# A linear-attention and gated-FFN kernel on one core: new engine orders, PSUM banks, engine choices and weight-load order, with the same operations

## The chip, the cores and the metric

The kernel runs on one core of one Trainium2 chip. The metric is the device time of one execution in microseconds (us), as the median of several runs of the same program. TensorE (PE in the profile, with PEld for its weight loads) multiplies matrices into PSUM. PSUM is used as eight banks of 128 x 512 f32. VectorE (DVE), ScalarE (ACT) and GpSimd (POOL) do elementwise work, and SyncE (SP) issues DMAs. Each engine takes its own list of instructions strictly in order and waits on semaphores for what other engines or DMAs must have done.

## The reference

Two layers follow each other. The first is a recurrence over 768 tokens for each of 4 batches and 8 heads of width 48. The second is a gated feed-forward layer (FFN) on the 3072 tokens of width 384 that come out of it, with a hidden width of 1536.

```python
f = 1.0 / (1.0 + np.exp(-f_logit))
for t in range(S):
    state = f[:, :, t, :, None] * state + np.einsum('bhd,bhe->bhde', k[:, :, t], v[:, :, t])
    y[:, :, t] = np.einsum('bhd,bhde->bhe', q[:, :, t], state)
x = y.transpose(0, 2, 1, 3).reshape(B * S, H * D)
out = (np.maximum(x @ w_gate, 0.0) * (x @ w_val)) @ w_out
```

Inputs and outputs are f32; the kernel multiplies in bf16.

## The kernel before, in words

**Units.** The tokens are cut into 12 units of 256 tokens: unit u is one batch and one pair of 128-token chunks (called y = 0 and 1), and units 0 to 3 are the first pair of the four batches, 4 to 7 the second, 8 to 11 the third. For each unit `unit` (the block from line 545 on) does the recurrence in chunks:

- four loads from DRAM, f, k, q and v, 384 KB each, issued by SyncE (`load`, DMA on line 468), into a ring of four buffers per input;
- on ScalarE the exponential (L546) and logarithm (L550, or L555 without the sum) of the gate, for some units a sum of pairs on GpSimd or VectorE (L552), then cumulative sums as matmuls (`cum`, L560 to 564) and exponentials of those (L577, L580, L587);
- the "hats", k and q times these exponentials (L599 for whole tiles in units 0 to 3, L605 for half tiles in the others);
- bf16 copies of v into `vpad` (L622; named v00, v01, v10, v11 by chunk and half) and, in units 0 to 3, into `vrest` (L626; named r0, r1). A copy goes through `copy_on`, whose line in the profile tells the engine: L402 ScalarE, L403 VectorE or GpSimd, L400 a reduction over one element on VectorE;
- the transposes of the hats: on TensorE for units 0 to 3 (L637, one for k, one for q, each with a copy out of PSUM, L643, named tk and tq), by two DMA transposes on SyncE's queue for units 4 to 11 (L648);
- the scores (L662) with their masks: on VectorE straight from PSUM (L676), or on ScalarE and then GpSimd (L671, L673);
- the decay of the state (L699 to 708, or through small DMAs in later units), the state matmuls k times v (L717 in units 4 to 11, L727 in 0 to 3), and the new state (L513, or L517 on VectorE and L520 on GpSimd);
- the output of each chunk, directly in transposed form (L760, copy named x0 or x1 into `xT`, L782) or in natural form (L767, L771) with a DMA transpose (L790).

**FFN.** Two units give a group of 512 tokens, that is four token tiles; there are six groups. `ffn_hidden` does one 128-wide slice j of the hidden layer: three matmuls with `wg` and three with `wv` (one line, L811), the relu on ScalarE (L816), the product on VectorE (L823). I call the three matmuls on one weight, with one PSUM tile, a matmul group. In the first two FFN groups the slices 0 to 5 are done for token tiles 0 and 1 and for tiles 2 and 3 apart, 256 columns each; all else has 512 columns. `ffn_out` multiplies by `wo` (L841, 12 matmuls to a token tile), copies out of PSUM (named o0 or o1) and stores (L862, SyncE). The last token tile is done in two cuts of columns, 256 and 128.

**Weights.** Each of the three weights is loaded in four slices of three 128-wide blocks, by DMAs that GpSimd issues (`load_w`, L482) and that cast from f32 to bf16. wg0 and wv0 hold what hidden slices 0 to 2 need, wg1 and wv1 slices 3 to 5, and so on. `FIRST` (L276) lists all loads of the start; a name after @ is a load that must have landed before the weight's DMA is issued (its release). Between the weights' issues GpSimd does its elementwise work in the order of its list.

**The order.** Nothing is scheduled at run time. The program adds 1088 operations, numbered 0 to 1087 in the order of the code. `SEQUENCE` (L184) gives, for each engine, the operations in the order in which it takes them; `HOMES` (L233) gives the PSUM tiles that each of the eight banks holds, one after the other; `UNITS` (L261) gives the engine of each elementwise operation of a unit. `Plan.link` finds what depends on what, `Plan.follow` lays the tiles into the banks, so that a tile's first matmul waits for the last reader of the tile before it, and `Plan.needs` works out the semaphore waits. `FILLERS` (L259) names TensorE operations that are preceded by matmuls on zeros, into a bank that is free at that time: (count of 512 columns, bank, columns of one more). `run` (L904) emits each engine's list.

Operations to which the lists below and the steps refer:

| number | what it is |
|---|---|
| 67, 68 / 105, 106 | cumulative sums of unit 0 / 1 on TensorE |
| 83, 85 / 121, 123 | transposes of k and q of unit 0 / 1; 84, 86 and 122, 124 are the copies tk, tq |
| 77 to 82 | v00, v01, r0, v10, r1, v11 of unit 0; 115 to 120 the same of unit 1 |
| 87, 90 / 125, 128 / 264, 268 | scores of unit 0 / 1 / 2 |
| 95, 134, 436 | state matmuls of unit 0, 1, 4 |
| 96, 99 / 135, 138 | outputs of unit 0 / 1 on TensorE; 97, 100 and 136, 139 their copies x0, x1 |
| 131 | the mask of unit 1 on GpSimd (L673) |
| 53, 54, 55, 56, 57 | the issues of wg0, wv0, wg1, wv1, wg2 (up to 60: wv2, wg3, wv3) |
| 146, 154 / 174, 178 | first hidden groups on tiles 0 and 1 / on tiles 2 and 3 |
| 194 | the first matmul group on wg2 (hidden slice 6) |
| 145, 424, 425 | v load of unit 4, and its two DMA transposes (L648) |
| 1083, 1086 | the last matmul group of the kernel and the last copy out of PSUM |

Of the kernel before, what the change touches and what calls it, by code (L numbers as in the profile page):

```python
# [38 lines left out]
class Plan:  # L39
# [91 lines left out]
    def needs(self):  # L131
# [127 lines left out]
FILLERS = {67: (9, 0, 448), 105: (6, 0, 320), 85: (0, 1, 448), 87: (2, 1, 256), 123: (2, 7, 0), 95: (1, 2, 0)}  # L259
# [23 lines left out]
def bass_hgrn2_outer__then__ffn_reglu_kernel(  # L283
# [601 lines left out]

    for n in FILLERS:
        pl.ops[n].reads.append("zeros")
# [73 lines left out]
```

## Time and profile before

| | |
|---|---|
| median of three runs | 187.22 us (186.69 to 187.68) |
| the profiled execution | 186.4 us |
| its span, first to last instruction | 185.1 us |
| granted TensorE clock | 1.00 |
| HBM read, written | 25.96 MB, 4.73 MB |
| DMA queues: SyncE's (q1), GpSimd's (q0) | 29.09 MB, 3.54 MB |

The span is what the profiler saw between the first and the last instruction; the 1.3 us to the execution's time lie outside it. The page lists for each engine its busy time, its share of the span and its count of instructions; the groups are by source line, with "xN" the count, then the summed busy time, the mean in ns of one, and the idle time of the engine just before them with what ended most of it. In the chain of waits each row is a start in us from the span's start, a duration, the engine, the tile and the line. In the list of instructions each row is a start and a duration too. In the table by stretches the numbers of each engine are its busy us and its count of instructions in that stretch. A wait is written reader, arrow, what ended it, then the summed idle us, the count and the largest.

### The profile page before, as it was taken

What the parts mean: (1) busy time and instruction counts of PE and PEld (TensorE: products, weight loads), DVE (VectorE), ACT (ScalarE), POOL (GpSimd) and SP (SyncE); (2) the same over time, 40 slices, a digit from 0 to 9 for tenths busy, and PEclk for the clock granted to TensorE, in tenths of its full rate; (3) what the DMA queues carried; (4) which work ended last, traced back from release to release, by engine and by line L of the source; (5) the groups of instructions that cost most, each with busy time, mean ns of one, the idle gap of its engine ahead of it and who ended that gap; (6) DMA issues with size and microseconds to landing.
All of it is one profiled execution on the core that took longest, in us unless ns stands there. A gap on an engine that the chain in (4) does not pass through costs nothing.

```text
span 185.1 us, 4315 instructions
## 1 busy us (share of the span) xinstructions
PE 180.1 (97%) x1689; PEld 102.9 (56%) x1689; DVE 126.1 (68%) x239; ACT 120.4 (65%) x242; POOL 101.2 (55%) x133
## 2 busy tenths in 40 slices
PE   7998998999999999999999999999999999999995
PEld 2454885476676556445565444656545566444564
DVE  3389775978488998999778696862865642335521
ACT  4999857889766888977786586266753641446112
POOL 5279903899949837979639998233670270000000
PEclk9999999999999999999999999999999999999999
DMA  5999999959999999979998998997028104000053
GB/s 153 323 325 267 226 204 205 251 123 175 197 302 202 211 264 289 242 162 262 266 230 159 261 258 188 234 172 178 17 67 217 22 4 106 0 0 4 0 212 127
DMA packets 83167, 32.89 MB, mean 178 GB/s; under 512 B 75334, under 2 KB 83148, under 8 KB 83148
## 3 DMA queue, kind: packets, MB, share of 16 engines
q1 hardware_dynamic: 78348, 29.09, 65.1%
q0 software_dynamic: 4800, 3.54, 12.7%
q8 instruction: 13, 0.21, 0.5%
q14 instruction: 6, 0.05, 0.1%
HBM read 25.96 MB, written 4.73 MB: 166 GB/s over the span
## 4 chain that ended last, share of the span: by engine, by line
PE 88%; SPq 3%; DVE 3%; DMA 3%; ACT 2%; issue 1%
PE ps L811 50%; PE ps L841 26%; SPq L468 3%; PE ps L662 3%; DMA k_in<-in_k_dram 3%; PE ps L760 2%; DVE ptm L676 1%; PE ps L771 1%; PE ps L717 1%; PE ps L767 1%; PE ps L637 1%; PE ps L562 1%; PE ps L727 1%; ACT relu L816 1%; DVE hats L599 1%
## 5 line engine op out<-in xcount | busy, mean ns | idle before, releaser
L823 DVE TENSOR_TENSOR gT<-relu,ps 128x512 bf16<-128x512 bf16 (+1 forms) x84 | 50.1, 625 | 24.6 <-PE ps L811 18.1
L816 ACT ACTIVATE relu<-ps 128x512 bf16<-128x512 f32 (+1 forms) x84 | 42.8, 537 | 29.1 <-PE ps L811 20.5
L811 PE MATMUL ps<-xT,wv 128*128 128x512 bf16 (+1 forms) x252 | 55.4, 349 | 0.0
L811 PE MATMUL ps<-xT,wg 128*128 128x512 bf16 (+1 forms) x252 | 54.6, 349 | 0.5 <-ACT f_in L550 0.5
L841 PE MATMUL ps<-wo,gT 128*128 128x384 bf16 (+2 forms) x300 | 53.7, 320 | 0.0
L841 PEld LDWEIGHTS ps<-wo,gT 128*128 128x128 bf16 x300 | 27.9, 98 | 18.0
L811 PEld LDWEIGHTS ps<-xT,wg 128*128 128x128 bf16 x252 | 23.2, 98 | 20.9 <-ACT f_in L550 0.8
L811 PEld LDWEIGHTS ps<-xT,wv 128*128 128x128 bf16 x252 | 23.3, 98 | 19.9 <-ACT relu L816 0.5
L673 POOL TENSOR_TENSOR ptm<-ptm,seen 128x512 bf16<-128x512 bf16 x21 | 24.0, 1156 | 18.1 <-ACT ptm L671 17.5
L605 POOL TENSOR_TENSOR hats<-q_in,expo 64x384 bf16<-64x384 f32 x28 | 27.8, 994 | 10.1 <-ACT expo L580 6.8
L676 DVE TENSOR_TENSOR ptm<-ps,seen 128x512 bf16<-128x512 f32 x27 | 17.5, 684 | 2.8 <-PE ps L662 2.6
L605 DVE TENSOR_TENSOR hats<-k_in,ps 64x384 bf16<-64x384 f32 x32 | 17.6, 551 | 0.9 <-DMA k_in<-in_k_dram 0.3
L520 POOL TENSOR_TENSOR st<-ssum,dec 128x384 bf16<-128x384 f32 x16 | 13.1, 832 | 5.5 <-DVE ssum L517 5.4
L671 ACT ACTIVATE ptm<-ps 128x512 bf16<-128x512 f32 x21 | 11.6, 595 | 6.0 <-PE ps L662 6.0
L403 DVE COPY osb<-ps 128x384 f32<-128x384 f32 (+2 forms) x15 | 7.9, 530 | 8.7 <-PE ps L841 8.4
L580 ACT ACTIVATE expo<-ps 128x384 f32<-128x384 f32 x22 | 9.9, 490 | 3.9 <-DVE ps L569 3.8
L403 POOL CAST vpad<-v_in 64x384 bf16<-64x384 f32 x20 | 10.4, 522 | 2.9 <-DMA v_in<-in_v_dram 1.8
L402 ACT ACTIVATE osb<-ps 128x384 f32<-128x384 f32 x10 | 4.9, 492 | 10.9 <-PE ps L841 10.9
L546 ACT ACTIVATE f_in<-f_in 128x768 f32<-128x768 f32 x12 | 10.1, 844 | 2.0 <-DMA f_in<-in_f_logit_dram 2.0
L402 ACT ACTIVATE vpad<-v_in 64x384 bf16<-64x384 f32 x21 | 10.9, 519 | 0.3
L552 POOL TENSOR_TENSOR bneg<-f_in 128x384 bf16<-128x384 f32 x7 | 7.0, 999 | 6.7 <-ACT f_in L550 6.6
L517 DVE TENSOR_TENSOR ssum<-ps,st 128x384 f32<-128x384 f32 x16 | 8.9, 554 | 2.2 <-PE ps L717 1.8
(90 smaller groups left out, 176.8 us busy)
## 6 DMA issues: line engine op xcount, KB each, us to landing
f_in<-in_f_logit_dram SPq DMA_DIRECT2D x12, 384.0 KB, 4.8
k_in<-in_k_dram SPq DMA_DIRECT2D x12, 384.0 KB, 4.8
q_in<-in_q_dram SPq DMA_DIRECT2D x12, 384.0 KB, 4.9
v_in<-in_v_dram SPq DMA_DIRECT2D x12, 384.0 KB, 5.3
out_dram<-osb SPq DMA_DIRECT2D x22, 192.0 KB, 2.2
wg<-in_moe_w_gate_dram POOLq DMA_DIRECT2D x4, 288.0 KB, 8.6
wv<-in_moe_w_val_dram POOLq DMA_DIRECT2D x4, 288.0 KB, 10.5
wo<-in_moe_w_out_dram POOLq DMA_DIRECT2D x4, 288.0 KB, 4.9
```

The costliest lines, as they stand in the source:

```text
L402: return sc.activation(out, src, AF.Copy)
L403: return engine[e].tensor_copy(out, src)
L520: add(e, lambda: engine[e].tensor_tensor(t4(s_new), t4(tmp), rate, ALU.mult), [key] + dk, [f"S{b}_{y}"], **(dict(occ=0.79, lat=0.1) if e = ...
L546: add("ACT", lambda: sc.activation(raw["f"], raw["f"], AF.Exp, scale=-1.0), [f"f{li}"], [f"f{li}"], **act_t(2 * HD))
L605: op = add(e, lambda i=i, n=n, x=x, e=e, y=y, lo=lo, exps=exps: engine[e].tensor_tensor(hats[64 * i:64 * i + 64, hi, y, x, :, 0:D], by_i[n ...
L671: add("ACT", lambda pt=pt, s=sj[j]: sc.activation(pt, s.ap[:, :].rearrange("p (n t) -> p n t", n=NP), AF.Copy), [sj[j]], [f"raw{mis[y]}_{j ...
L673: add("POOL", lambda pt=pt, mask=mask: gp.tensor_tensor(pt, pt, mask, ALU.mult), [f"raw{mis[y]}_{j}", "seen"], [f"raw{mis[y]}_{j}", f"ptm{ ...
L676: add("DVE", lambda pt=pt, mask=mask, s=sj[j]: ve.tensor_tensor(pt, s.ap[:, :].rearrange("p (n t) -> p n t", n=NP), mask, ALU.mult), [sj[j ...
L811: mm = te.matmul(bank.ap[:, 0:n], wt[:, kt, j * 128:(j + 1) * 128], xT[xi][:, kt, n0:n1], start=(kt == 0), stop=(kt == NK - 1))
L816: add("ACT", lambda: sc.activation(relu[ri][:, n0:n1], gate.ap[:, 0:n], AF.Relu), [gate], rk, **act_t(n))
L823: return ve.tensor_tensor(o, a, b, ALU.mult)
L841: mm = te.matmul(bank.ap[:, 0:cut[1] - cut[0]], gT[gi][:, j, r * C:(r + 1) * C], wo[:, j, cut[0]:cut[1]], start=(j == 0), stop=(j == NJ - 1))
```

## The change

The same 1088 operations are added, by the same functions. Five tables at the top of the file are replaced: the order on each engine (`SEQUENCE`), the tiles of each bank (`HOMES`), the zeros-matmuls (`FILLERS`), the engine of 73 elementwise operations (`UNITS`), and the releases of the weights (`FIRST`). Of the 73 operations 22 go from VectorE to ScalarE, 14 from ScalarE to GpSimd, 12 from ScalarE to VectorE, 10 from GpSimd to VectorE, 10 from GpSimd to ScalarE and 5 from VectorE to GpSimd. The lists then hold 247 operations on ScalarE (before: 241), 234 on VectorE (239), 128 on GpSimd (129), and 359 on TensorE and 120 on SyncE as before. The zeros-matmuls are 25 instead of 24.

In the first unit v00, v01, v10 and the product q0 go to GpSimd, v11 to ScalarE and the product k1 to VectorE; in the second v01 and r0 go to GpSimd, v11, r1, tk, o0, o1 and x1 to ScalarE, v10 and the product q1 to VectorE. In units 2 to 11 it is some of the copies named v, r, tk, o0, o1, x0 and x1, and the sum (L552) of units 3, 5, 6 and 8.

The diff, cut to the starts of the lists, the fillers, two units and the loads:

```diff
@@ -183,97 +183,98 @@
     "PE": [
-        36, 67, 68, 105, 106, 83, 85, 132, 87, 123, 121, 90, 93, 95, 125, 96, 128, 134, 273, 244, 245, 135, 99, 138, 262, 146, 174, 170, 178,
-        150, 154, 156, 152, 180, 172, 148, 176, 260, 186, 162, 182, 158, 166, 190, 164, 160, 188, 184, 192, 194, 264, 268, 198, 168, 318, 202,
...
-        1059, 1077, 1071, 1072, 1073, 1078, 1079, 1060, 1061, 1080, 1081, 1082, 1083],
+        36, 68, 67, 106, 105, 83, 85, 123, 87, 132, 90, 121, 93, 128, 95, 96, 125, 245, 99, 244, 134, 135, 273, 138, 154, 146, 262, 178, 174,
+        170, 150, 176, 156, 148, 152, 260, 172, 166, 182, 180, 186, 162, 158, 184, 190, 188, 168, 268, 264, 164, 194, 198, 192, 202, 160, 318,
...
+        1060, 1046, 1061, 1047, 1067, 1072, 1073, 1078, 1079, 1080, 1081, 1082, 1083],
     ],
     "ACT": [
-        10, 65, 66, 103, 69, 73, 104, 70, 74, 107, 108, 111, 84, 112, 79, 80, 78, 124, 133, 77, 94, 116, 242, 117, 243, 97, 130, 246, 250, 136,
-        274, 100, 147, 175, 171, 247, 251, 155, 151, 179, 187, 163, 159, 167, 183, 191, 287, 288, 195, 266, 269, 271, 199, 203, 292, 319, 293,
...
+        65, 66, 103, 10, 104, 69, 73, 74, 70, 107, 111, 112, 84, 108, 82, 124, 242, 122, 79, 94, 243, 130, 97, 119, 120, 133, 246, 100, 250, 136,
+        247, 274, 139, 251, 175, 179, 171, 155, 151, 147, 261, 167, 183, 163, 187, 191, 159, 287, 269, 288, 266, 195, 271, 319, 203, 292, 199,
...
     ],
     "POOL": [
-        3, 8, 33, 0, 6, 9, 7, 4, 32, 20, 1, 30, 31, 21, 75, 82, 114, 81, 53, 54, 115, 119, 120, 118, 55, 56, 131, 57, 58, 102, 59, 34, 35, 60,
-        289, 270, 272, 259, 255, 267, 299, 295, 61, 62, 300, 303, 301, 63, 302, 64, 315, 407, 317, 282, 141, 328, 451, 414, 419, 465, 464, 459,
...
+        0, 1, 33, 3, 8, 20, 6, 4, 9, 31, 30, 21, 7, 72, 80, 77, 53, 81, 54, 78, 32, 116, 117, 115, 55, 131, 56, 57, 34, 58, 59, 35, 60, 102, 272,
+        270, 255, 259, 256, 267, 299, 295, 61, 62, 304, 63, 64, 315, 317, 141, 407, 282, 328, 414, 419, 465, 459, 464, 458, 467, 466, 423, 421,
...
     ],
     "SP": [
-        37, 41, 38, 39, 43, 40, 42, 44, 45, 47, 46, 49, 48, 50, 51, 142, 52, 283, 323, 143, 144, 285, 284, 286, 145, 424, 425, 329, 471, 470,
...
+        37, 41, 38, 39, 43, 42, 40, 45, 47, 44, 46, 49, 48, 50, 51, 52, 142, 283, 323, 143, 144, 285, 284, 286, 424, 425, 145, 329, 471, 470,
...
-FILLERS = {67: (9, 0, 448), 105: (6, 0, 320), 85: (0, 1, 448), 87: (2, 1, 256), 123: (2, 7, 0), 95: (1, 2, 0)}
+FILLERS = {68: (9, 0, 448), 106: (3, 0, 448), 83: (2, 0, 448), 85: (3, 0, 192), 123: (1, 2, 0), 128: (3, 7, 0)}
-    0: {'kps': False, 'qps': False, 'q0': 'DVE', 'q1': 'DVE', 'even': 'PE', 'm00': 'DVE', 'm01': 'DVE', 'm10': 'DVE', 'tk': 'ACT', 'm11': 'DVE', 'r1': 'POOL', 'tq': 'DVE', 'v11': 'POOL', 'v10': 'ACT', 'r0': 'ACT', 'v01': 'ACT', 'v00': 'ACT', 'vb': 'DVE1', 'pr': False, 'o1': 'ACT', 'vc0': 'DVE', 'x0': 'ACT', 'x1': 'ACT', 'yy': True, 'o0': 'ACT', 'vc1': 'ACT', 'td': False, 'k0': 'DVE', 'k1': 'POOL'},
+    0: {'kps': False, 'qps': False, 'q0': 'POOL', 'q1': 'DVE', 'even': 'PE', 'm00': 'DVE', 'm01': 'DVE', 'm10': 'DVE', 'tk': 'ACT', 'm11': 'DVE', 'r1': 'POOL', 'tq': 'DVE', 'v11': 'ACT', 'v10': 'POOL', 'r0': 'ACT', 'v01': 'POOL', 'v00': 'POOL', 'vb': 'DVE1', 'pr': False, 'o1': 'ACT', 'vc0': 'DVE', 'x0': 'ACT', 'x1': 'ACT', 'yy': True, 'o0': 'ACT', 'vc1': 'ACT', 'td': False, 'k0': 'DVE', 'k1': 'DVE'},
-    1: {'kps': True, 'r0': 'ACT', 'm01': 'DVE', 'm00': 'DVE', 'tq': 'ACT', 'v11': 'POOL', 'even': 'PE', 'tk': 'DVE', 'q1': 'POOL', 'v00': 'POOL', 'm11': 'POOL', 'r1': 'POOL', 'm10': 'DVE', 'v01': 'ACT', 'v10': 'POOL', 'q0': 'DVE', 'qps': False, 'yy': False, 'td': False, 'vb': 'DVE', 'vc0': 'DVE', 'o0': 'DVE', 'vc1': 'DVE', 'x0': 'ACT', 'o1': 'DVE', 'x1': 'DVE'},
+    1: {'kps': True, 'r0': 'POOL', 'm01': 'DVE', 'm00': 'DVE', 'tq': 'ACT', 'v11': 'ACT', 'even': 'PE', 'tk': 'ACT', 'q1': 'DVE', 'v00': 'POOL', 'm11': 'POOL', 'r1': 'ACT', 'm10': 'DVE', 'v01': 'POOL', 'v10': 'DVE1', 'q0': 'DVE', 'qps': False, 'yy': False, 'td': False, 'vb': 'DVE', 'vc0': 'DVE', 'o0': 'ACT', 'vc1': 'DVE', 'x0': 'ACT', 'o1': 'ACT', 'x1': 'ACT'},
...
-FIRST = 'f0 k0 q0 v0 f1 k1 q1 v1 f2 k2 q2 v2 f3 k3 q3 v3 wg0 wv0@k1 wg1@q1 wv1 wg2@q2 wv2@k2 wg3@f0 wv3@f2 wo0@f2 wo1@k1 wo2@v1 wo3@v2'
+FIRST = 'f0 k0 q0 v0 f1 k1 q1 v1 f2 k2 q2 v2 f3 k3 q3 v3 wg0 wv0 wg1@v0 wv1 wg2@q1 wv2 wg3@k1 wv3@q2 wo0 wo1@f3 wo2@f2 wo3@k3'
```

In the new list of GpSimd the mask of unit 1 (131) stands between the issues of wg1 (55) and wv1 (56); in the old one it stands behind wv1. In the new list of TensorE the scores of unit 2 (268, 264) stand ahead of the first group on wg2 (194); in the old one they stand behind it. In the new list of SyncE the v load of unit 4 (145) stands behind that unit's two transposes (424, 425). The last four operations of TensorE's list (1080 to 1083) are the same in both.

More of the change, by code (lines that the diff above doesn't have):

```diff
@@ new lines @@
+    7: {'v10': 'ACT', 'kps': True, 'q1': 'POOL', 'v01': 'DVE1', 'q11': 'POOL', 'm00': 'DVE', 'v11': 'DVE1', 'even': 'DVE', 'm10': 'POOL', 'm11': 'DVE', 'm01': 'POOL', 'q10': 'POOL', 'qps': False, 'q01': 'POOL', 'q0': 'POOL', 'o0': 'ACT', 'x1': 'ACT', 'td': True, 'x0': 'DVE', 'o1': 'DVE', 'v00': 'ACT', 'sum': 'POOL'},
+    8: {'m10': 'DVE', 'v11': 'DVE1', 'q01': 'POOL', 'm01': 'POOL', 'even': 'DVE', 'q0': 'POOL', 'v10': 'POOL', 'q1': 'POOL', 'm00': 'DVE', 'kps': True, 'q11': 'POOL', 'q00': 'POOL', 'qps': False, 'v00': 'POOL', 'q10': 'POOL', 'v01': 'DVE1', 'pr': False, 'td': True, 'x0': 'ACT', 'o1': 'DVE', 'x1': 'ACT', 'o0': 'ACT', 'sum': 'POOL'},
@@ L274 @@
+    11: {'q0': 'DVE', 'v01': 'DVE1', 'q10': 'POOL', 'm00': 'DVE', 'q01': 'POOL', 'm11': 'POOL', 'q1': 'POOL', 'q00': 'POOL', 'kps': True, 'v11': 'ACT', 'm01': 'DVE', 'q11': 'POOL', 'even': 'DVE', 'v00': 'ACT', 'm10': 'POOL', 'v10': 'ACT', 'yy': True, 'o1': 'ACT', 'td': True, 'x0': 'ACT', 'x1': 'ACT', 'o0': 'ACT', 'sum': 'POOL'},
 }
 SLICES = {'wg': [3, 3, 3, 3], 'wv': [3, 3, 3, 3], 'wo': [3, 3, 3, 3]}
[L276 removed]
+FIRST = 'f0 k0 q0 v0 f1 k1 q1 v1 f2 k2 q2 v2 f3 k3 q3 v3 wg0 wv0 wg1@v0 wv1 wg2@q1 wv2 wg3@k1 wv3@q2 wo0 wo1@f3 wo2@f2 wo3@k3'
```

46 lines of the change are left out of this document (21 added, 25 removed), and 72 rows, old and new, of tables (SEQUENCE, UNITS).

## The prediction

> **What bounds the kernel now.** I read the page first, then the busy time by stretches, then the chain of waits in order of time, then TensorE's own waits, then the queues of ScalarE and GpSimd at the start.
>
> ```profile
> span 185.1 us, 4315 instructions
> ...
> PE 180.1 (97%) x1689; PEld 102.9 (56%) x1689; DVE 126.1 (68%) x239; ACT 120.4 (65%) x242; POOL 101.2 (55%) x133
> ```
>
> ```profile
> 0.00:20.39 20.39, 17.93 (x256) 9.58 (x257) 13.40 (x39) 17.11 (x33) 12.95 (x33) 1.00 1.06 263
> 20.39:37.00 16.61, 16.02 (x148) 10.51 (x145) 12.39 (x27) 12.27 (x30) 8.33 (x12) 1.00 1.21 222
> 37.00:183.10 146.10, 146.10 (x1292) 82.79 (x1288) 100.03 (x174) 91.06 (x180) 79.89 (x89) 1.00 0.70 161
> 10.00:20.00 10.00, 9.12 (x214) 5.59 (x212) 9.03 (x17) 9.77 (x21) 9.04 (x13) 1.00 1.21 280
> ```
>
> The columns after the width are busy time and count of TensorE, its weight loads, VectorE, ScalarE and GpSimd, then the granted clock, the DMA share and GB/s. From 37 us to the last matmul TensorE has no idle time at all: 146.10 of 146.10. Since ends of matmuls are modelled, I check the pace on the chain:
>
> ```profile
> 20.56 3.93 PE ps L811 x36
> 28.31 0.85 ACT f_in L550
> 29.27 0.81 PE ps L811 x3
> 132.00 8.42 PE ps L811 x39
> 157.82 12.95 PE ps L811 x60
> 183.18 0.29 DVE osb L403
> ```
>
> 39 matmuls in 8.42 us are 216 ns each, and 60 in 12.95 us, in the stretch where the other engines have little left to do, are 216 ns too. So TensorE runs at its own pace while the others are busiest: **after 37 us there is nothing to gain from an order, only something to lose.** What an order can win lies before 37 us. There TensorE waits like this:
>
> ```profile
> PE ps L811 <- ACT f_in L550: 0.5, 1, 0.5
> PEld ps L811 <- DMA wv<-in_moe_w_val_dram: 0.3, 1, 0.3
> ```
>
> ```profile
> 25.76 1.15 PE L811 MATMUL ps<-xT,wg 128*128 128x256 bf16 x9
> 26.95 1.81 PE L811 MATMUL ps<-xT,wv 128*128 128x256 bf16 x15
> ```
>
> ```profile
> 16.47 0.78 POOL L482 DMA_DIRECT2D wg<-in_moe_w_gate_dram  x1
> 17.24 0.78 POOL L482 DMA_DIRECT2D wv<-in_moe_w_val_dram  x1
> 18.13 1.15 POOL L673 TENSOR_TENSOR ptm<-ptm,seen 128x512 bf16<-128x512 bf16 x1
> 19.24 0.80 POOL L482 DMA_DIRECT2D wg<-in_moe_w_gate_dram  x1
> ```
>
> The time to landing of these three weight slices (wg1, wv1, wg2), each asked for alone:
>
> ```profile
> DMA to landing us min/median/max: 7.2/7.2/7.2
> ```
> ```profile
> DMA to landing us min/median/max: 9.7/9.7/9.7
> ```
> ```profile
> DMA to landing us min/median/max: 9.9/9.9/9.9
> ```
>
> wg1 lands at 16.47+7.2 = 23.7, wv1 at 17.24+9.7 = 26.9, wg2 at 19.24+9.9 = 29.1. TensorE starts the first matmul on wv1 at 26.95 and the first on wg2 at 29.27, each just after the landing. The list blames ScalarE's line 550 for the second wait (0.5). That is the logarithm of unit 3, which no line-811 matmul reads; it ended at 28.31+0.85 = 29.16 by chance. So **the weight stream sets the pace until 29.3 us**, and TensorE had 0.5 us to spare there.
>
> **The change, part by part.** TensorE keeps its 1,689 matmuls but for one more filler (25 zeros-matmuls for 24), SyncE its 120 issues. The fillers run while TensorE waits in the first 17 us; one that outlasts its wait costs at most its own 0.22 (512 columns, pace above), which is inside the head's bounds. 73 elementwise operations change engine, nearly as many onto each engine as off it (ScalarE +6, VectorE -5, GpSimd -1).
>
> *Head, on ScalarE.* It is full: 9.77 of 10 us from 10 to 20 us. Its prices:
>
> ```profile
> L402 ACT ACTIVATE vpad<-v_in 64x384 bf16<-64x384 f32 x21 | 10.9, 519 | 0.3
> L402 ACT ACTIVATE xT<-ps 128x384 bf16<-128x384 f32 x9 | 4.9, 604 | 1.1 <-PE ps L760 1.1
> L402 ACT ACTIVATE qkT<-ps 128x1024 bf16<-128x1024 bf16 x3 | 3.1, 1035 | 0.1
> L587 ACT ACTIVATE ps<-ps 128x384 f32<-128x384 f32 x22 | 10.2, 492 | 0.0
> ```
>
> ```profile
> 19.51 0.64 ACT L402 ACTIVATE xT<-ps 128x384 bf16<-128x384 f32 x1
> 20.06 0.59 DVE L403 CAST xT<-ps 128x384 bf16<-128x384 f32 x1 [0.31 <-PE ps L760]
> ```
>
> Five copies of v go (unit 0's v00, v01, v10; unit 1's v01, r0): 5 x 0.519 = 2.6. Three come (v11 of units 0 and 1, r1 of unit 1), with unit 1's key transposition copy tk and its x1: 3 x 0.519 + 1.035 + 0.604 = 3.2. Net +0.6. The hidden layer on token tiles 2 and 3 waits for unit 1's x1, so far ready on VectorE at 20.06+0.59 = 20.65. Now it is ScalarE's, behind all that ended with unit 0's x1 at 19.51+0.64 = 20.15, and behind one exponential of unit 2 (0.49): 20.15+0.6+0.49 = 21.2. Meanwhile TensorE can do two groups on tiles 0 and 1 and unit 2's query transposition, which stood there before as well. A group of three is 3.93/12 = 0.33 us. The third group stood at 20.56+2x0.33 = 21.2 on the chain, which counts a group from where the one before has drained (20.56, for an issue at about 20.4); issued at 21.3 it stands at 21.5: 0.3 late. Bounds: 0 (VectorE and GpSimd have less to do, so ScalarE's inputs come earlier) to 1.2 (twice the net, if unit 1's v copies, now late on ScalarE, hold its state matmuls). I take 0.3, and the spare 0.5 us before 29.27 swallows it: **0**, or up to 0.7. If that cover were gone, it would cost its 0.3.
>
> *Weight releases.* The names after @ hardly bind (each load they name has landed or is far ahead); GpSimd's own order does. Unit 1's mask (1.15) now stands before wv1 instead of behind it: wv1 starts at 17.24+1.15 = 18.4 at best, and at 18.13+1.15 = 19.3 if the mask must wait as long as it does now, 1.2 to 2.0 later; wg2 follows it, 0 to 0.8 later than 19.24. Both have lain 9 us in line so far, in a stretch with DMA share 1.21, so most of a later issue is hidden by the line; without that cover the whole shift counts. Bounds for the landing of wg2: -0.5 (TensorE's wait there is gone and no more can be won) to +0.8; wv1 alone up to +2.0. I take **+0.3**, near the end at which the line covers it. The Trainium skill's "DMA: Bandwidth & Descriptors", section "Queues, rings and completion order", says that each DMA engine goes round the queues that have work, packet by packet. By that rule time in which GpSimd's ring is empty goes to SyncE's loads and is not given back, which speaks against the change; no row here shows how full the ring is, so the trace neither bears it out nor speaks against it.
>
> *Work put ahead of the wait.*
>
> ```profile
> 30.08 0.55 PE ps L662 x16
> ```
>
> Unit 2's scores (0.55) now run before the first group on wg2 instead of behind it; in exchange one value group (0.33) falls behind. While TensorE waits for wg2 it has done 0.2 more: **-0.2**.
>
> *After 37 us.* I looked for loads and copies pushed behind others. The clearest is unit 4, whose v load now stands in SyncE's queue behind its two transpositions:
>
> ```profile
> 51.42 3.89 SPq L468 DMA_DIRECT2D v_in<-in_v_dram  x2
> 55.42 3.56 SPq L648 DMA_TRANSPOSE qkT<-hats  x2
> ```
> ```profile
> DMA to landing us min/median/max: 3.6/5.3/15.4
> ```
> ```profile
> L403 POOL CAST vpad<-v_in 64x384 bf16<-64x384 f32 x20 | 10.4, 522 | 2.9 <-DMA v_in<-in_v_dram 1.8
> ```
> ```profile
> 62.99 0.50 PE L717 MATMUL ps<-vpad,hats 128*128 128x96 bf16 x8
> ```
>
> The transpositions wait for unit 4's hats and keep about their start. The two took 3.56 us to issue with one load more ahead of them; at 2 to 3.56 the v load is issued at 57.4 to 59.0. It lands 3.6 to 5.3 later (least and median of all 12 v loads), and two copies in a row on GpSimd (2 x 0.52) follow: 62.0 at best, 65.3 at worst; the state matmuls stand at 62.99. Wait: 0 to 2.3. I take **+0.3**, near the least, since fewer bytes lie ahead of it than of a usual v load. For the other moves I take 0: VectorE is busy 100, ScalarE 91 and GpSimd 80 of 146 us, and TensorE's order keeps at least 0.8 us of other matmuls between each result and its reader in both versions (counted along the lists by the pace above). That cover is gone where a queue's head waits; the third rival prices it.
>
> *Tail.* The last four TensorE groups are the same. The last copy (128 columns) moves from VectorE (0.29) to ScalarE, which the trace shows for 16 columns and for 384:
>
> ```profile
> L708 ACT ACTIVATE dec<-ps 128x16 f32<-128x16 f32 x7 | 1.3, 183 | 0.5 <-PE ps L703 0.5
> L402 ACT ACTIVATE osb<-ps 128x384 f32<-128x384 f32 x10 | 4.9, 492 | 10.9 <-PE ps L841 10.9
> ```
>
> Between 0.18 and 0.49, so -0.1 to +0.2; nearer 16 columns than 384, **0**.
>
> **Sum.** 0 + 0.3 - 0.2 + 0.3 + 0 = +0.4 us. The profiled execution took 186.4 (span 185.1 and 1.3 around it), 0.8 under the median of 187.22 of the runs shown. I carry the difference over: 186.4 + 0.4 = 186.8 under the profiler, **187.6** as a median. Half a per cent (0.94 us) is about what a measurement of this kernel tells from no change: 186.3 to 188.2 counts as the same.
>
> **Rivals.**
> 1. *The forecast*, about the same: chance 0.50, own range 186.3 to 188.2. For it: one bound before 29.3 us, which neither order owns, and none but TensorE's pace after it.
> 2. *The weights come late.* The ring runs empty while the mask holds up wv1, and SyncE's loads take the engines meanwhile. wv1 lands 2.0 later, at 28.9; five groups (5 x 0.33) and the scores (0.5) stand between it and wg2, so the latter starts at 31.0 instead of 29.27, and the 0.2 comes off: +1.5, with unit 4's 0.3 not less: 187.22+1.5 to +1.8 = 188.7 to 189.0. It decides from about 1 us of late landing on. For it: the mask is before wv1. Against: 9 us in line. Chance 0.22; slower. (The rule of the Trainium skill above is this case's.)
> 3. *A queue's head waits in the second part*, at unit 4 (up to 2.3) or at others of the kind in the reordered SyncE and GpSimd queues: +1.0 to +2.5, 188.2 to 189.7. Against it: the 0.8 us and more. Chance 0.13; slower.
> 4. *The weights come sooner, or just in time.* Both waits go (0.3 and 0.5), 0.2 is won, unit 4 loses nothing: -1.0, 186.2. For it: VectorE and GpSimd have less to do in the head. Against: the same bytes through DMA engines with no room. Chance 0.15; faster.
>
> The change doing nothing at all (187.2) lies inside the first case. Range for 8 in 10: 186.2 (fourth case) to 189.2 (second case and most of the third). Faster 0.15, same 0.50, slower 0.22 + 0.13 = 0.35.
>
> **What would show it.** Right: the first line-811 matmuls on tiles 2 and 3 near 21.3; wv1 issued at 18.4 to 19.3; the first matmul on wg2 at 29.2 to 29.8, just after its landing; ScalarE still near 10 of 10 from 10 to 20; no wait of TensorE over 0.3 after 37 us but for unit 4's state. Wrong: hidden work starting 1 us late with weights already there (the head is bound by ScalarE); wg2 landing after 30; idle time in 37 to 183; or all of it an even 0.8 us or more earlier from 30 us on.

## The result and the profile after

The changed kernel took 189.86 us (median of 12 runs, 187.82 to 191.25), the kernel before 186.61 in as many runs beside it (186.15 to 187.68). The ratio is 1.0139, with a 95% interval of 1.0115 to 1.0164. It leaves out every run that is over 1.5% above the fastest of its kernel, so the medians of a kernel that scatters lie further apart (1.0174) than its ratio says. The forecast was 187.6, in a range of 186.2 to 189.2: the change is slower by 3.25 us between the medians, not by 0.4.

The profiled execution took 189.29 us. Its page starts with the span and the busy times. Then comes TensorE by stretches (columns as in the prediction); the last fence is the same stretch of the kernel before.

```profile
span 188.1 us, 4330 instructions
...
PE 180.1 (96%) x1690; PEld 103.5 (55%) x1690; DVE 124.2 (66%) x234; ACT 122.1 (65%) x248; POOL 99.8 (53%) x132
```
```profile
37.00:100.00 63.00, 62.94 (x699) 37.91 (x698) 51.61 (x95) 50.42 (x105) 49.21 (x56) 1.00 1.04 224
100.00:112.00 12.00, 12.00 (x62) 5.85 (x60) 9.17 (x16) 9.43 (x20) 7.35 (x8) 1.00 0.81 209
112.00:126.00 14.00, 11.43 (x113) 6.43 (x111) 8.48 (x15) 5.41 (x10) 10.88 (x14) 1.00 0.93 187
126.00:182.00 56.00, 56.00 (x386) 30.08 (x385) 28.16 (x45) 23.88 (x47) 12.31 (x12) 1.00 0.26 64
```
```profile
112.00:126.00 14.00, 14.00 (x138) 8.02 (x136) 10.43 (x18) 6.90 (x15) 7.28 (x9) 1.00 0.98 192
```

TensorE's busy time is 180.1 in both pages, and the span is 3.0 longer. In this trace all of that stands in one stretch, 112 to 126 us, with 11.43 of 14.00 busy and 113 matmuls where the kernel before did 138. Up to there nothing is lost: if each matmul is counted at the pace that its kind keeps back to back (216 ns for 512 columns) and the zeros-matmuls are left out, 18.5 us of the first 112 are not matmul time in either trace (18.53 after, 18.49 before). After 112 us TensorE's list of waits names two, and the list of its instructions shows where (at the end of a row, in brackets, stands the idle time before it and what ended that):

```profile
PE ps L768 <- POOL ptm L674: 1.5, 1, 1.5
...
PE ps L718 <- POOL vpad L404: 1.1, 1, 1.1
```
```profile
117.64 0.33 PE L718 MATMUL ps<-vpad,hats 128*128 128x96 bf16 x4 [1.10 <-POOL vpad L404]
117.91 0.62 PE L663 MATMUL ps<-qkT 48*128 48x128 bf16 x16
...
123.01 0.33 PE L768 MATMUL ps<-st,qkT 128*128 128x96 bf16 x4 [1.45 <-POOL ptm L674]
```

Lines below the tables are one higher in the changed file (L717 is now L718). Unit 8's state waits 1.10 for its v copy v10, and unit 8's first output 1.45 for its mask; from start to start, less the matmuls' own time, the two cost 1.26 and 1.61. Both come from GpSimd. Here is its list at that time:

```profile
107.45 0.50 POOL L404 CAST vpad<-v_in 64x384 bf16<-64x384 f32 x1
113.80 3.13 POOL L606 TENSOR_TENSOR hats<-q_in,expo 64x384 bf16<-64x384 f32 x3 [5.85 <-DMA q_in<-in_q_dram]
117.00 1.06 POOL L404 CAST vpad<-v_in 64x384 bf16<-64x384 f32 x2
118.03 0.82 POOL L521 TENSOR_TENSOR st<-ssum,dec 128x384 bf16<-128x384 f32 x1
118.93 2.07 POOL L606 TENSOR_TENSOR hats<-q_in,expo 64x384 bf16<-64x384 f32 x2
121.07 0.50 POOL L404 CAST vpad<-v_in 64x384 bf16<-64x384 f32 x1
121.72 1.15 POOL L674 TENSOR_TENSOR ptm<-ptm,seen 128x512 bf16<-128x512 bf16 x1
```

GpSimd sits 5.85 us at a product of **unit 10** (914), whose q load (665) has not landed. Behind it in its list stand the copy of **unit 8** (758, first of the pair at 117.00), whose v load had landed at 103.7, and the mask of unit 8 (765, at 121.72). The mask's own input was ready at 118.95, after the scores that the late copy had held up; then it stood 2.8 us behind the work that had piled up on GpSimd. The load is late because of its place on SyncE. These are all issues of SyncE from 99.8 to 111 us, and then the one row of that load in the kernel before, with the time from issue to landing of each (after, before):

```profile
99.87 0.58 SPq L863 DMA_DIRECT2D out_dram<-osb  x1
100.49 0.29 SPq L684 DMA_DIRECT2D rates<-expo  x1
100.83 1.42 SPq L863 DMA_DIRECT2D out_dram<-osb  x1
102.30 1.38 SPq L469 DMA_DIRECT2D v_in<-in_v_dram  x1
103.72 0.58 SPq L469 DMA_DIRECT2D k_in<-in_k_dram  x1
104.41 2.54 SPq L649 DMA_TRANSPOSE qkT<-hats  x1
107.00 0.43 SPq L684 DMA_DIRECT2D rates<-expo  x1
107.90 1.87 SPq L863 DMA_DIRECT2D out_dram<-osb  x3
109.81 0.46 SPq L469 DMA_DIRECT2D q_in<-in_q_dram  x1
110.31 0.70 SPq L693 DMA_DIRECT2D dec<-rates  x1
```
```profile
101.11 0.59 SPq L468 DMA_DIRECT2D q_in<-in_q_dram  x1
```
```profile
DMA to landing us min/median/max: 3.9/3.9/3.9
```
```profile
DMA to landing us min/median/max: 4.7/4.7/4.7
```

Each row starts 0.04 to 0.5 us after the one before ended: SyncE issues almost without a pause (9.55 of the 10.40 us up to 110.27 are issue time). In such a queue a place is a time: ten more entries stand ahead of this load than before, two fewer, and it is issued 8.7 us later. The load's own transfer takes no longer (3.9 against 4.7). The queue was nearly full before as well: of the 43 us from 88 to 131, issues took 36.8 before and 39.4 after.

### The profile page after: what moved, and what is told of

Its sections match the earlier page's. It is cut to its first block, busy times and chain, and to the rows that moved or that the text cites. A ratio compares the mean times of both kernels' runs of the same rounds, so it can differ in the third digit from the quotient of the medians.

```text
span 188.1 us, 4330 instructions
## 1 busy us (share of the span) xinstructions
PE 180.1 (96%) x1690; PEld 103.5 (55%) x1690; DVE 124.2 (66%) x234; ACT 122.1 (65%) x248; POOL 99.8 (53%) x132
## 4 chain that ended last, share of the span: by engine, by line
PE 80%; DVE 5%; issue 4%; DMA 3%; POOL 3%; ACT 3%; SPq 0%; POOLq 0%
PE ps L812 46%; PE ps L842 23%; PE ps L663 3%; PE ps L761 2%; DVE ptm L677 2%; DMA f_in<-in_f_logit_dram 2%; POOL hats L606 2%; DVE hats L600 1%; PE ps L772 1%; DMA dec<-rates 1%; PE ps L768 1%; PE ps L718 1%; PE ps L638 1%; ACT f_in L547 1%; PE ps L563 1%
## 5 line engine op out<-in xcount | busy, mean ns | idle before, releaser
L812 PE MATMUL ps<-xT,wv 128*128 128x512 bf16 (+1 forms) x252 | 56.2, 349 | 0.0
L842 PE MATMUL ps<-wo,gT 128*128 128x384 bf16 (+2 forms) x300 | 53.1, 320 | 0.0
L403 ACT ACTIVATE osb<-ps 128x384 f32<-128x384 f32 (+2 forms) x19 | 8.8, 471 | 13.7 <-PE ps L842 13.6
L404 POOL CAST vpad<-v_in 64x384 bf16<-64x384 f32 x19 | 9.5, 502 | 2.7 <-DMA v_in<-in_v_dram 1.7
L588 ACT ACTIVATE ps<-ps 128x384 f32<-128x384 f32 x22 | 10.9, 501 | 0.0
L600 POOL TENSOR_TENSOR hats<-q_in,expo 128x384 bf16<-128x384 f32 x5 | 5.1, 1030 | 9.4 <-ACT expo L581 6.4
L403 ACT ACTIVATE xn<-ps 128x384 bf16<-128x384 f32 x9 | 4.4, 491 | 8.2 <-PE ps L772 7.9
```

Source lines behind the costliest of these rows:

```text
L403: return sc.activation(out, src, AF.Copy)
L588: add("ACT", lambda i=i, ex=ex: sc.activation(bc[i].ap[:, 0:HD] if in_place else ex[:, 1, :], bc[i].ap[:, 0:HD], AF.Exp, scale=1.0), [bc[i ...
L812: mm = te.matmul(bank.ap[:, 0:n], wt[:, kt, j * 128:(j + 1) * 128], xT[xi][:, kt, n0:n1], start=(kt == 0), stop=(kt == NK - 1))
L842: mm = te.matmul(bank.ap[:, 0:cut[1] - cut[0]], gT[gi][:, j, r * C:(r + 1) * C], wo[:, j, cut[0]:cut[1]], start=(j == 0), stop=(j == NJ - 1))
```

## Experiments

Theory: SyncE's list, nearly full from about 88 to 131 us, was given an order in which urgent entries stand behind others, and the heads of the other queues, GpSimd's above all, pass the delay on to work that was ready. (The head of a queue is the entry that is next; while it waits, nothing behind it starts.) Rivals: the transfers themselves collide; GpSimd has too much to do after the moves; or there are many single places without slack. Each edit moves entries of a list, given by their numbers (`+` new place, `-` old place); the difference in us is between medians of the kernel and of the kernel before on the same chip.

**The change once more** (no edit).

> The changed kernel once more, for the size of its loss on this chip and a second trace. Every theory: 1.0 to 1.7% over the kernel before (2.0 to 3.2 us). In the trace all theories expect the same two waits of TensorE between 112 and 125 us (1.1 and 1.45 in the first trace, together 2.5). If the loss stands in other places this time, the first trace was an accident.

190.18 us, +3.4; ratio 1.0177 (1.0140 to 1.0213). The trace has unit 8's waits again (0.42 and 1.46, counted from start to start as above), but also 1.40 at the start of the fourth FFN group and 0.59 at unit 7's output, and the first matmul on wg2 at 30.26 instead of 29.40. The two new waits are at queue heads too. The group waits for unit 7's output transposes in SyncE's queue; the output waits for a bank that a relu has to read, and ScalarE came late to that relu because it sat at a gate load (f_in) that had not landed:

```profile
90.44 0.84 ACT L547 ACTIVATE f_in<-f_in 128x768 f32<-128x768 f32 x1 [1.12 <-DMA f_in<-in_f_logit_dram]
```

So the first trace was no accident, and not the whole loss either. What made the weights late is taken up with the head below.

**One or two entries of SyncE back.**

```diff
 "SP": 493, 239, 769, 503,
+665,
 666, 664, 760, 815, 540, 241, 521,
-665,
 817, ...
```

> The changed kernel with one entry of SyncE's list moved: unit 10's q load stands ahead of that unit's v load again, as in the kernel before, so that it is issued near 102 instead of 109.8 us. Theory A (this load alone: GpSimd sits 5.9 us at unit 10's product q01, with unit 8's v copy v10 and mask behind it): both waits go, +0.0 us to the kernel before (186.3 to 186.9). Theory B (two late entries in one queue: unit 8's second transposition lands at 117.40, and the scores that follow the state in TensorE's list need it): the wait of 1.45 goes, but TensorE still waits about 0.8 to 1.0 at unit 8's scores instead of its state, +0.8 to +1.1 us. Theory C (the transfers collide, so an earlier issue lands no earlier): q lands after 110 and 1.5 to 3 us of the loss stay.

188.85 us, +2.0; 1.0126 (1.0078 to 1.0174). The load is issued at 102.04 and both old waits are gone; TensorE now waits at unit 8's scores, for the transposition that lands at 118.52:

```profile
PE ps L663 <- issue: 1.2, 1, 1.2
PE ps L768 <- DVE ssum L518: 0.8, 1, 0.8
```

That is theory B's new wait, a little larger than it said, and a second one (0.8, at unit 8's second output) follows that no theory had, with 0.5 at unit 7's output. So the time (+2.0) is above what A and B gave; C's size fits, but not its reason, for the load landed at 107.7.

```diff
 "SP": ... 521, 665,
+761,
 817, 807, 784,
-761,
 651, ...
```

> The changed kernel with one entry of SyncE's list moved: unit 8's second transposition (761) stands directly behind unit 10's q load, three entries earlier, so that it is issued near 110.4 instead of 113.2 us and lands near 114; the q load keeps its late place. Theories A and B: nothing is won, since the copy v10 still comes at 117.5 on GpSimd and the mask at 122.9: +2.3 to +3.2 us over the kernel before. A theory in which the transposition alone is the cause: the loss falls under 1 us.

189.43 us, +2.6; 1.0142 (1.0103 to 1.0181). Nothing certain is won, as A and B said; unit 8's mask is still late (1.2), and the fourth group's start waits 1.4.

> The changed kernel with both entries moved: unit 10's q load ahead of its v load, unit 8's second transposition ahead of the small transfer for unit 9's decay. Theories A and B: no wait of TensorE over 0.3 us after 37 us and the time of the kernel before, -0.3 to +0.3 us. Theory B is told from A by the difference to the kernel with the q load alone (0.8 to 1.1 under B, 0 under A). Theory C, or a theory that GpSimd has too much to do after the move of copies: over +1.0 us is left.

188.06 us, +1.2; 1.0050 (1.0012 to 1.0088), with runs from 186.19 to 190.67. Two entries win back 2.1 of the 3.4 us on that chip. The forecast of no rest was wrong:

```profile
PE ps L768 <- DVE ssum L518: 1.2, 1, 1.2
```

Unit 8's second output needs a bank that VectorE has still to read for unit 9 (822). VectorE waits for unit 7's new state on GpSimd (662, done at 123.20), which stands behind unit 8's (777), which waits for a small transfer that lands at 121.46 (771). Three queues in a row, each blocked at its head.

**GpSimd's list**, together with the two moves on SyncE.

```diff
 "POOL": 756, 914, 908, 800, 758, 802, 611,
+662,
 915, 909, 919, 765, 777,
-662,
```

> The changed kernel with the two SyncE entries moved (unit 10's q load, unit 8's second transposition) and one entry of GpSimd's list: unit 7's new state ahead of unit 10's products and of unit 8's new state, whose small transfer lands at 121.5. In the trace with the two SyncE moves a wait of 1.4 us was left at unit 8's second output, whose bank VectorE had still to read for unit 9, and VectorE waited for unit 7's state. Theory of the chain: that wait goes and with it 1.0 to 1.4 us, down to the kernel before, -0.2 to +0.4. Rival (the next queue head takes its place): over +0.8 us stays.

191.91 us, +5.3, with runs from 189.33 to 193.04; 1.0220 (1.0171 to 1.0269): the rival. In the trace, of a run of 192.94, unit 7's own small transfer (651) lands at 120.14, so GpSimd sits there, and unit 8's mask behind it:

```profile
120.21 0.83 POOL L521 TENSOR_TENSOR st<-ssum,dec 128x384 bf16<-128x384 f32 x1 [4.45 <-DMA dec<-rates]
```

TensorE waits 2.87 us for that mask. From 1.15 us after it goes on, its granted clock is 0.50 for 3.41 us, and a matmul of 384 columns takes 320 ns there instead of 162: some 1.7 us more (an estimate, half of the 3.41) that are not in the wait itself. After the 1.45 of the first trace the clock stayed at 1.00.

With the state directly ahead of unit 8's instead (`765, 662, 777`):

> The changed kernel with three entries moved: on SyncE unit 10's q load and unit 8's second transposition earlier, as before, and on GpSimd unit 7's new state directly ahead of unit 8's (it stood directly behind), so that VectorE's read for unit 9, which frees the bank of unit 8's second output, no longer waits for unit 8's late small transfer. Theory of the chain: the wait of 1.4 us that was left there goes, and the time falls by 0.8 to 1.4 us against the two moves on SyncE alone, to +0.2 to +0.9 us over the kernel before; what stays is a wait of 0 to 1.4 us at the start of the fourth FFN group, for unit 7's output transposes. Rival (unit 7's state is itself late by its own small transfer, as when it stood ahead of unit 10's products): over +1.5 us.

187.68 us, +1.2; 1.0056 (1.0036 to 1.0076). The wait at unit 8 is gone; 0.53 at the fourth group's start and 0.95 at unit 10's cumulative sums (for a bank that ScalarE has still to read) are left.

SyncE as changed, and only GpSimd mended (`756, 800, 758, 802, 611, 914, 908, ... 765, 662, 777`):

> The changed kernel with GpSimd's list alone mended, SyncE's as changed: unit 10's products q01 and q00 stand behind unit 9's product, unit 8's and unit 9's v copies and unit 6's state, and unit 7's new state directly ahead of unit 8's. The q load still lands at 113.7. Theory of the blocked head (the late load costs time only through what stands behind its reader on GpSimd): the wait at unit 8's state and the one at its mask go; the late transposition (landing at 117.4) still holds unit 8's scores for 0.8 to 1.0; together -1.4 to -2.2 us against the changed kernel, so +0.8 to +1.8 over the kernel before. Theory that the late load costs time by itself, for unit 10: less than 0.7 us is won.

187.89 us, +1.4; 1.0063 (1.0038 to 1.0089). The load is as late as ever (it lands at 114.27), both old waits at unit 8 are gone, and 2 us are won: it cost its time through what stood behind its reader. The late transposition shows, a little smaller than expected (0.63 at unit 8's scores). Two more waits in this trace, 1.37 at unit 10's cumulative sums and 0.83 at 134 us, were in no theory.

**Unit 11's k load (782)**, which the change put ahead of unit 7's output transposes (655, 609, 660). Back behind unit 8's output transposition (780), alone and together with the three moves above:

> The changed kernel with one entry of SyncE's list moved: unit 11's k load stands behind unit 8's output transpose, as in the kernel before, instead of ahead of unit 7's output transposes. Theory (each entry ahead of its place in a full queue costs its issue time to all behind it): everything on SyncE from 94 to 124 us comes about 0.6 to 1.1 earlier, unit 10's q load too, and the loss falls by 0.5 to 1.3 us, to +1.7 to +2.6 us over the kernel before; both waits at unit 8 stay, smaller. If its 384 KB were only bytes among others, it would win less than 0.3 us.

188.27 us, +1.5; 1.0073 (1.0048 to 1.0098): by the ratios it wins 1.2 us against the first measurement of the changed kernel and 1.9 against the second, so as much as forecast or more. The trace, of the slowest run, doesn't show where.

> The same three moves, and unit 11's k load behind unit 8's output in SyncE's list again, as in the kernel before, instead of ahead of unit 7's output transposes. Theory (four entries out of place explain the loss): no wait of TensorE over 0.4 us after 37 us, except where a weight is late before 31 us; -0.3 to +0.4 us to the kernel before. Rival (the orders have no slack in many more places, so that each trace shows another wait): +0.8 us or more, with single waits at new places.

187.35 us, +0.8, with runs from 185.64 to 188.64; 1.0014 (0.9985 to 1.0043). By the ratio no loss can be told any more; by the median some is left, and the trace has waits at other places (1.28 at the fifth group's start, 0.61 at unit 7).

**The same entries in the kernel before.** Unit 10's q load alone about ten entries later; then that, the k load early and the transposition late:

> The kernel before with the one load (unit 10's q) about ten entries later in SyncE's list, as in the changed kernel. It lands near 113.5 instead of 105.8 us, GpSimd waits some 3 us at unit 10's product and its later work shifts by as much; unit 8's v copy then ends near 118.6 for a state that stands at 119.1, and its mask near 119.8 for an output at 119.8. All theories: 0 to +0.5 us. The same edit would then cost nothing here, where TensorE's list asks for unit 8 1.5 us later, and over 1 us in the changed kernel. Over +1.0 us: the load's place alone decides in any order.

186.75 us, +0.2; 1.0015 (0.9996 to 1.0034). The load is issued 7.4 us later and costs nothing that these runs can tell, as forecast. GpSimd waits 2.24 us for it instead of 5.85, and TensorE has no wait at unit 8.

> The kernel before with three entries of SyncE's list at places like the new ones: unit 11's k load ahead of unit 7's output transposes, unit 10's q load some ten entries later, unit 8's second transposition ahead of unit 11's v load. All else is as before. Theory S: these alone cost time, by hand +0.5 to +1.5 us: q lands near 114, GpSimd's four products of unit 10 come about 4 later, unit 8's v copy behind them at 118.9 for a state at 119.1, and its mask at 120.6 for an output at 119.8. Theory G (the loss needs the new GpSimd order): +0.3 or less.

187.76 us, +1.2; 1.0060 (1.0032 to 1.0088). The size is as forecast, the place is not: the one large wait is at the fourth group's start, for unit 7's output transposes, which were issued behind the k load and landed at 102.7 and 103.1:

```profile
PE ps L811 <- DMA xT<-xn: 1.5, 1, 1.5
```

**SyncE's whole old list** in the changed kernel:

> The changed kernel, but SyncE's whole list (120 issues) as in the kernel before; every other list, bank and engine choice stays new. Theory S (SyncE's order is the whole cause; the heads of the other queues only pass its delays on): unit 10's q load lands before 107, the small transfers for the decays of units 7 and 8 before 104 and 120, no wait of TensorE over 0.4 us after 37 us, and the time of the kernel before, -0.3 to +0.4 us. Theory G (the new lists of GpSimd and VectorE lose time of their own, by unit 7's new state standing behind unit 8's): 1.0 us or more over the kernel before stay, with a wait near unit 8's second output.

195.60 us, +9.0; 1.0461 (1.0423 to 1.0499). Both theories failed: S in the time, G in the place and the reason. The old list suits the old lists of the others: here ScalarE sits at an output copy whose buffer a store on SyncE has not yet emptied, and a relu that TensorE needs stands behind it:

```profile
112.89 0.49 ACT L403 ACTIVATE osb<-ps 128x384 f32<-128x384 f32 x1 [4.97 <-DMA out_dram<-osb]
```

TensorE's wait of 3.39 us for that relu is again followed by 3.41 us at a granted clock of 0.50 (the second row here; the first is the stretch of the wait), in which a matmul of 512 columns takes 427 ns instead of 216:

```profile
110.20:113.90 3.70, 0.33 (x2) 0.00 (x0) 1.09 (x2) 1.01 (x3) 0.00 (x0) 1.00 1.16 299
114.63:118.04 3.41, 3.41 (x10) 1.26 (x9) 1.28 (x2) 1.82 (x6) 3.17 (x4) 0.50 0.05 9
```

The statement "SyncE's order is the cause" is too short, then: it is SyncE's order against the others. The waits that the trace lists do not add up to the whole 9.0.

**The head.** First the mask ahead of wv1, alone, in the kernel before (`55, 131, 56`):

> The kernel before with one entry of GpSimd's list moved: unit 1's mask ahead of the issue of wv1, so that wv1 is issued near 19.2 instead of 17.24 and wg2 near 20.0 instead of 19.24. If the line of transfers covers it (wv1 still lands near 27.0, wg2 near 29.2): 0 to +0.2 us. If GpSimd's ring runs empty meanwhile: wv1 lands 1 to 2 later, and +0.8 to +1.5 us.

186.94 us, +0.4; 1.0030 (1.0009 to 1.0050). wv1 is issued at 19.16 and lands at 27.05, wg2 at 19.96 and 29.20: the line of transfers covers it. The little loss is not at the weights: the first matmul on wg2 is at 29.34 (29.27 before), and the trace has a wait of 0.8 at 86.3 us instead.

Then the order of SyncE's first loads. In the changed kernel unit 0's v stands behind unit 1's k, and unit 1's v behind unit 2's f and q:

```diff
 "SP": 37, 41, 38, 39, 43,
-40, 42, 44, 45, 47,
+42, 40, 45, 47, 44,
```

Unit 1's v landed at 12.82 before, at 15.16 in the first trace after, and at 16.66 in the second, where GpSimd waited for it with the issue of wg1 behind (from 16.47 before to 18.25):

```profile
16.79 0.50 POOL L404 CAST vpad<-v_in 64x384 bf16<-64x384 f32 x1 [0.93 <-DMA v_in<-in_v_dram]
17.35 0.50 POOL L404 CAST vrest<-v_in 64x384 bf16<-64x384 f32 x1
17.80 0.50 POOL L404 CAST vpad<-v_in 64x384 bf16<-64x384 f32 x1
18.25 0.78 POOL L483 DMA_DIRECT2D wg<-in_moe_w_gate_dram  x1
```

Of the eleven traces with that order up to then, four had unit 1's v at 15.8 to 16.7 and the first matmul on wg2 at 30.2 to 30.7; the other seven had v at 15.1 to 15.3 and that matmul at 29.3 to 29.7.

> The kernel before with the first 15 issues of SyncE (the loads of units 0 to 3) in the changed kernel's order: unit 0's v behind unit 1's k, unit 1's v behind unit 2's f and q. All else is as before. Unit 1's v lands at 15.2 to 16.7 instead of 12.8; three of its copies stand on GpSimd ahead of the issue of wg1, which comes at 17.3 to 18.8 instead of 16.5, and the issues of wv1 and wg2 by as much later. Theory (the late v holds GpSimd and with it the weights): the first matmul on wg2 at 29.4 to 30.4 instead of 29.3, +0.2 to +0.9 us. Theory that the line of transfers covers it: under +0.2 us.

187.37 us, +1.2; 1.0053 (1.0032 to 1.0073). wg1 is issued at 17.67 and lands at 26.65, and wg2's first matmul is at 30.63. The mechanism is as forecast; its price (0.6 to 1.4 by the interval) reaches above the 0.9.

> The changed kernel with the first 15 issues of SyncE in the order of the kernel before; all else stays changed. Theory: unit 1's v lands at 12.8, the issue of wg1 comes near 16.7, wg2 is there by 29.4 in nearly all executions, and of the loss 0.2 to 0.7 us goes; the waits near unit 8 stay (+2 to +3 us over the kernel before). If the head has no part in the loss: no difference to the changed kernel (+2.6 to +3.3 us).

188.37 us, +2.2; 1.0118 (1.0092 to 1.0143). Between 0.4 and 1.1 of the loss go (by the ratios of the two measurements of the changed kernel), about as forecast, and unit 8's mask still costs 1.55 in the trace. wg2 lands at 29.24 there, but TensorE comes to it only at 30.04, so this trace doesn't show where the time was won.

**All together.** First seven entries, with the head as changed; then four of them (those of the kernel at 187.35) with the head's old order:

> The changed kernel with seven entries moved: on SyncE unit 10's q load, unit 8's second transposition, unit 11's k load and one small transfer for unit 10's decay (which stood ahead of unit 9's output transposes); on GpSimd unit 10's first two products behind unit 8's and unit 9's copies, and unit 7's state ahead of unit 8's. Theory (these entries are the whole loss): 186.2 to 187.0, -0.3 to +0.5 us to the kernel before, and no wait of TensorE over 0.5 us after 37 us. Rival (no slack in many places of the new lists): +0.8 us or more, with a wait at a place that no entry here touches.

188.20 us, +1.4; 1.0046 (1.0017 to 1.0074): the rival in the time. The place, though, was touched: the 0.89 at unit 10's scores is for a copy on ScalarE that waits until unit 8's first output transposition (775) has landed, at 128.77, and this edit puts the k load (782) directly ahead of that entry. In the kernel at 187.35, where 782 stands behind 780, it landed at 127.25.

> The kernel with the four entries moved (unit 10's q load, unit 8's second transposition, unit 11's k load on SyncE, unit 7's state on GpSimd; 187.35 us) and SyncE's first 15 issues in the order of the kernel before as well. Theory (SyncE's list, in its head and between 90 and 131 us, is the loss): 186.5 to 187.1 and a narrower spread, with no run over 188.3. Rival (the rest is scattered in single places without slack): no change, 187.2 to 187.8, and a spread of 3 us as before.

186.91 us, +0.7 (186.19 to 188.52); 1.0037 (1.0013 to 1.0061). The median is in the forecast, the spread above it. Its trace has no wait over 0.4 us after 37 us, and the execution took 186.20, as the kernel before:

```profile
PE ps L448 <- DVE zeros L391: 1.3, 1, 1.3
PE ps L564 <- ACT bneg L556: 1.0, 2, 0.8
PE ps L638 <- DVE hats L600: 0.6, 2, 0.4
```

So the four entries take away most of the loss, 2.5 of 3.3 us by the medians. The order of the first loads adds nothing to them that shows: +0.8 without it, +0.7 with it, and by the ratios 1.0014 against 1.0037. Nor do the single gains add up; moved alone, each entry wins part of the same time. What the head costs in the changed kernel stays open: alone it costs 1.2 in the kernel before, but in all three traces of the changed lists with the old head (`a_old_sync`, `a_head`, `mend_head`) TensorE comes to wg2 at 30.0 to 30.1, 0.8 to 0.9 after it has landed.

Of the rivals, the collision of transfers falls for the load in question (its own transfer took no longer), and a GpSimd with too much to do is not what began it (it sat idle for 5.85 us). Single places without slack hold for the rest, 0.3 to 0.8 us: the traces of the mended kernels show waits that differ from one to the next, and which of them it is in the median run stays open. No version beat the kernel before.

## Why the prediction was wrong, step by step

The rows of after that answer to the steps (GpSimd's issue of wv1, the first matmul on wg2, unit 4's v load and state, the last copy; then the landing time of that v load):

```profile
18.96 0.80 POOL L483 DMA_DIRECT2D wv<-in_moe_w_val_dram  x1
```
```profile
29.40 1.46 PE L812 MATMUL ps<-xT,wg 128*128 128x512 bf16 x6
```
```profile
57.31 0.58 SPq L469 DMA_DIRECT2D v_in<-in_v_dram  x1
```
```profile
62.96 0.51 PE L718 MATMUL ps<-vpad,hats 128*128 128x96 bf16 x8
```
```profile
186.18 0.28 ACT L403 ACTIVATE osb<-ps 128x128 f32<-128x128 f32 x1 [0.29 <-PE ps L842]
```
```profile
DMA to landing us min/median/max: 4.1/4.1/4.1
```

- **Head on ScalarE (0): right in this trace, in part by luck.** The first matmuls on tiles 2 and 3 came at 21.74 (forecast 21.3), and 29.40 for wg2 is in 29.2 to 29.8. But it was not "just after its landing": wg2 had landed at 29.05, and TensorE came to it 0.35 later without an idle moment from 20 us on. The weights no longer set the pace there.
- **Mask and releases (+0.3): the weights lose nothing by the mask.** wv1 was issued at 18.96, inside 18.4 to 19.3, and landed at 26.92 (26.90 before). With the mask alone moved, wv1 was issued 1.9 us later and landed 0.15 later; that run's +0.4 is the size of the term, but its wait stands at 86 us and not at the weights. The fear had been that GpSimd's ring runs empty, by the Trainium skill's "DMA: Bandwidth & Descriptors", section "Queues, rings and completion order", where each DMA engine goes round the queues that have work. The landing speaks against an empty ring here; no row shows the ring itself. But the step looked only at GpSimd's order. It overlooked that unit 1's v load moved back on SyncE and that its copies stand ahead of wg1: late weights, the second rival (0.22), did come about (0.8 to 1.3 us later than in the first trace), by another mechanism than the one it named, in four of those eleven traces.
- **Unit 2's scores ahead of wg2 (-0.2): right in size.** At 32 us, counted as above, 14.55 us are not matmul time, against 14.87.
- **Unit 4's v load (+0.3): right in its working, 0 in size.** Issued at 57.31 (forecast 57.4 to 59.0), landed at 61.4, and the state at 62.96 has no wait in the list.
- **Tail (0): right.** The last copy took 0.28 instead of 0.29.
- **"For the other moves I take 0": this step failed.** Its reason was that TensorE's order "keeps at least 0.8 us of other matmuls between each result and its reader". That counts matmuls along TensorE's list, and no row of the prediction shows the count. It says nothing of results that become ready later because their own queue is held at its head: unit 8's copy and mask came 1.26 and 1.61 us after TensorE could have gone on. The third rival had the mechanism ("a queue's head waits in the second part") and was given 0.13 and +1.0 to +2.5; in the first trace it cost 2.9 (1.26 and 1.61), in the second 3.9 at four places, and the measured 189.86 lies even above that rival's 189.7. The sum of the other five terms was +0.4 and came out at 0.0 in the first trace.

The way to see it stood in the trace of before. The busy lines of a page leave out the issuing of DMAs, so no row says that SyncE is full; its queue listed as a timeline does, and it would have given for each moved entry the sum of the issue times that it is moved past, as it did for unit 4. Done for unit 10's q load, with ten entries more ahead of it and two fewer, that is 6.8 us by the issue times of before (it became 8.7), where GpSimd came to that load's first product 4.8 us after the landing (110.6 against 105.8):

```profile
110.62 4.21 POOL L605 TENSOR_TENSOR hats<-q_in,expo 64x384 bf16<-64x384 f32 x4
```

And in the new list the copy and the mask of unit 8 stand behind that product. I priced one such entry and took it for the worst. The base hid a part of the miss: the forecast started from 187.22, the median of three runs, where twelve gave 186.61; +0.4 on that would have been 187.0.

The Trainium skill's "DMA: Bandwidth & Descriptors", section "Rules for kernel authors", says that spreading DMAs over several engines saves only the issuing time of their sequencers. In the trace after, this time fills 39.4 of the 43 us on SyncE from 88 to 131, and the late load comes from it. No run tried to spread it, so what that would save is not shown.

## What to carry to other kernels

Where an order written out by hand fills a DMA queue, list that queue as a timeline first: a place in it is a time, and an entry moved back is late by about the sum of the issue times that it is moved past, whatever the transfer takes (6.8 by the old trace here, 8.7 measured; 7.7 and 7.4 for the same load in the kernel before). Then follow each late landing to its reader and look at what stands behind the reader in that engine's list, since ready work behind a blocked head was what TensorE waited for here. And an order is one thing across all queues: one load 7 us later cost nothing that shows in the old lists and was part of the loss in the new ones, and SyncE's good old list in the new kernel cost 9 us.

## What the runs showed of the hardware that was not expected

- The time that SyncE takes for one issue varies widely for the same kind of DMA. In the first trace after, a load of 384 KB mostly took 1.15 us back to back in the first 15 us, 3.0 to 5.5 from 15 to 32 us, and 0.46 to 1.9 from 88 to 131, most often 0.58; a DMA transposition took 1.2 to 2.5 there. What sets it is not shown.
- In the two traces with a TensorE wait of 2.87 and 3.39 us in mid-kernel, 3.41 us at a granted clock of 0.50 followed, beginning 1.15 and 0.71 us after the wait. After the waits of 1.10 and 1.45 in the first trace the clock stayed at 1.00. What lies between was not tried.
- Two executions of one program differ by over 1 us in when a load lands: unit 1's v, issued at 10.23 and 10.54, took 4.9 and 6.1 us. At its old place it landed at 12.7 to 13.3 in all seven traces, at its new one at 15.1 to 16.7 in twelve. The changed kernel scatters over 3.4 us, the kernel before over 1.5; that the landings are the reason is not shown.
